# Linear attention in token order, with DMA transposes and one pool of 28 buffers

## The chip, the cores and the metric

The kernel runs on one core of a Trainium2 chip. The metric is the device time of one execution in microseconds (us); the median of three runs of the kernel before is 790.57 us (790.43 to 791.24). All data are bfloat16 in and out, sums are float32.

## The reference

Four layers follow each other on 2048 tokens of 576 values: linear attention, MLP, attention, MLP, each with a layer norm in front and a residual around it. Both attentions share their weights, and so do both MLPs.

```python
def _A_ref(x, wqkv, wo):                      # 32 heads of 18
    qkv = (x @ wqkv) -> q, k, v
    phi = lambda t: where(t > 0, t + 1, exp(t)) + 1e-6
    kv = einsum("bhsd,bhse->bhde", phi(k), v)
    z = einsum("bhsd->bhd", phi(k))
    num = einsum("bhqd,bhde->bhqe", phi(q), kv)
    den = einsum("bhqd,bhd->bhq", phi(q), z)[..., None] + 1e-6
    return (num / den) reshaped to tokens x 576, @ wo
def _B_ref(x, w1, b1, w2, b2):                # 576 -> 4608 -> 576
    h = gelu(layernorm(x) @ w1 + b1)
    return h @ w2 + b2
x = x + _A_ref(layernorm(x)); x = x + _B_ref(layernorm(x))    # and once more
```

## The kernel before, in words

Tokens are worked on in 16 tiles of 128. All weights stay on chip; the rows x between layers go through a DRAM buffer x_d and come back into rings (x_ring).

**LN pipe.** LNPipe (lines 220 to 308) takes each tile through statistics (DVE), a power on GpSimd for 1/sigma, the normalised row y (DVE, GpSimd), and then five TensorE transposes into PSUM (line 297) and one copy (lines 299, 301) into yT, which holds the normalised tokens with the 576 values along the partitions. Every call of tick() moves each tile one stage on.

**Attention, layer_A (358 to 534).** Front half, per token tile: k (line 370) and v (382, 385) in token order, phi of k in two ScalarE passes (319, 321) and two DVE steps (322, 324), and the sum of kv over all tiles (400). q is computed in channel order, a group of 7 heads by 512 tokens at a time (406). z comes out of a ones column of v. Second half: kv is masked to its heads (429, 433), multiplied into wo (451), the denominators of four tiles come from short matmuls (466, 470), their reciprocals (474) are spread over the channels by a matmul (482), copied (484) and multiplied into phi(q) (485). The output product (493) then takes scaled phi(q) and kv-wo; residual() (342) adds x and stores the row.

**MLP, LayerB (545 to 651).** Four chunks of 512 tokens. The first product makes 36 blocks of 128 hidden channels in 9 groups of four (m1_group, 553). TensorE runs two 64-row halves at once: the upper half takes the blocks in the order 0, 1, 2, 3, the lower 2, 3, 0, 1. The 64 rows left over of the 576 (w_tail) add one matmul to one half of every block, so that block 0 is complete one step before block 2. evict (586) reads a complete block with ScalarE's GELU into hT; that of block 3 is held back into the next group. Two tiny ScalarE copies per group (relay, 598) keep the two halves from meeting in one PSUM bank. Where the four blocks lie:

```python
hps = [ps_h.tile([P, 512], F32, name="h_ps", tag="h") for _ in range(2)]
pair = ps_acc.tile([P, 2, 512], F32, name="hp_ps", tag=next_acc())
dst = [hps[0][:], pair[:, 0, :], hps[1][:], pair[:, 1, :]]
```

The second product (640) sums 36 blocks by 2 halves for each of the chunk's four tiles; while it runs, the next chunk's rows (or the next attention's) are normalised and transposed, one tile for each tick.

**What sets the order.** A scheduler lays out each engine's instructions and places the semaphore waits by the tiles that they read and write. pe() chains TensorE's instructions to the program's order in the MLP and the front half of attention. All DMAs are issued by SP, in one queue, in order.

Of the kernel before, what the change touches and what calls it, by code (L numbers as in the profile page):

```python
# [17 lines left out]
KD = 5  # L18
# [5 lines left out]
GO = [126 * g for g in range(G)]  # L24
EPS = 1e-5
# [6 lines left out]
C1 = 1.0 + 1e-6  # L32


def build(tc, A_x, A_wqkv, A_wo, B_w1, B_b1, B_w2, B_b2, out, dbg=None, n_layers=4):
    nc = tc.nc
    dbg = dbg or {}
    with ExitStack() as ctx:
        const = ctx.enter_context(tc.tile_pool(name="const", bufs=1))
        ps_h = ctx.enter_context(tc.tile_pool(name="ps_h", bufs=3, space=PSUM))  # L40
        ps_tp = ctx.enter_context(tc.tile_pool(name="ps_tp", bufs=1, space=PSUM))
        ps_acc = ctx.enter_context(tc.tile_pool(name="ps_acc", bufs=1, space=PSUM))
        dpool = ctx.enter_context(tc.tile_pool(name="dram", bufs=1, space=DRAM))

# [13 lines left out]
        maskz = const.tile([P, 7, DH], F32, name="maskz")  # L58
        head_sel = const.tile([P, G, H], BF16, name="head_sel")
        head_bc = const.tile([P, G, P], BF16, name="head_bc")  # L60
        quad_mask = const.tile([P, 4, P], BF16, name="quad_mask")
        z_row = const.tile([P, 1], BF16, name="z_row")
        eps_row = const.tile([1, H], BF16, name="eps_row")
        one_row = const.tile([1, P], BF16, name="one_row")
        act_dummy = const.tile([P, 1], F32, name="act_dummy")

        def select(tile_, fill, op, base, pattern, mult):
            return lambda: nc.gpsimd.affine_select(out=tile_, in_=tile_, compare_op=op, fill=fill, base=base,
                                                   pattern=pattern, channel_multiplier=mult)

        def fill(tile_, value):
            return lambda: nc.gpsimd.memset(tile_[:], value)

        def inner_diag(tile_, lead, n):
            return [fill(tile_, 1.0),
                    select(tile_[:], 0.0, ALU.is_ge, 0, lead(1) + [[-DH, n]] + ([[0, DH]] if tile_ is maskz else []), 1),
                    select(tile_[:], 0.0, ALU.is_ge, DH - 1,
                           lead(-1) + [[DH, n]] + ([[0, DH]] if tile_ is maskz else []), -1)]

        hb = head_bc[:, :, 0:126].rearrange("p g (h d) -> p g h d", h=7)  # L80
        mask_steps = inner_diag(maskz, lambda sign: [], 7) + [
            select(maskz[:], 1.0, ALU.not_equal, -126, [[0, 7], [0, DH]], 1),
            fill(z_row, 0.0),
            select(z_row[:], 1.0, ALU.not_equal, -126, [[0, 1]], 1),
            fill(eps_row, 1e-6),
            fill(one_row, 1.0),
        ] + inner_diag(head_sel, lambda sign: [[126 * sign, G]], H) + [
            fill(quad_mask, 1.0),
            select(quad_mask[:], 0.0, ALU.is_ge, 0, [[-32, 4], [0, P]], 1),
            select(quad_mask[:], 0.0, ALU.is_ge, 31, [[32, 4], [0, P]], -1),  # L90
            fill(head_bc, 0.0),
        ] + [select(hb, 1.0, ALU.not_equal, -32 * quad, [[-7, G], [-1, 7], [0, DH]], 1) for quad in range(4)]
# [7 lines left out]
        wo_sb = const.tile([126, G, D], BF16, name="wo_sb")  # L100
# [6 lines left out]
        kvT = const.tile([P, G, 126], BF16, name="kvT")  # L107
        zsel = const.tile([P, G, H], BF16, name="zsel")
        NY = 4
        y_ring = [const.tile([P, DPAD], BF16, name=f"y_ring{i}") for i in range(NY)]  # L110
        NV = 3
        v_ring = [const.tile([P, G, P], BF16, name=f"v_ring{i}") for i in range(NV)]
        NX = 5
        x_ring = [const.tile([P, D], F32, name=f"x_ring{i}") for i in range(NX)]
# [3 lines left out]
        blk = ctx.enter_context(tc.tile_pool(name="blk", bufs=NF))  # L118

        x0_tiles = {}  # L120
# [13 lines left out]
        pe_chain = dict(on=False, last=None)  # L134

        def pe(inst):
            if pe_chain["on"]:
                if pe_chain["last"] is not None:
                    tc.add_manual_dep(inst.ins, pe_chain["last"], NOSYNC, reason="TensorE order in the MLP")
                pe_chain["last"] = inst.ins.name  # L140
            return inst

        def load_x0(t):
            x0 = blk.tile([P, D], BF16, name="x0", tag="blk")
            chained(nc.sync.dma_start(out=x0[:], in_=x_in[t * P:(t + 1) * P, :]))
            x0_tiles[t] = x0
# [18 lines left out]
        for i in (NY - 1, 0, 1, 2):  # L165
            nc.vector.memset(y_ring[i][:], 0.0)
        warm_ps = ps_h.tile([P, 512], F32, name="warm_ps", tag="h")

        def warm_pe(n):
            for _ in range(n):  # L170
                pe(nc.tensor.matmul(warm_ps[:], lhsT=y_ring[NY - 1][:, 0:P], rhs=y_ring[NY - 1][:, 0:512],  # L171
                                    start=True, stop=True))
# [3 lines left out]
        for vr in v_ring:  # L176
            nc.gpsimd.memset(vr[:, 4, 72:126], 0.0)
            nc.gpsimd.memset(vr[:, :, 126:127], 1.0)
            nc.gpsimd.memset(vr[:, :, 127:128], 0.0)

        def piece_wo():
            chained(nc.sync.dma_start(out=wo_sb[:, 0:4, :], in_=A_wo[0:504, :].rearrange("(g p) n -> p g n", p=126)))
            chained(nc.sync.dma_start(out=wo_sb[0:72, 4, :], in_=A_wo[504:D, :]))
# [32 lines left out]
        state = dict(ycnt=0, vcnt=0, xl=0)  # L216
        pool_last = dict(norm=None)
        dve_last = dict(norm=None, sum=None, phi=None)

        class LNPipe:  # L220
# [3 lines left out]
            def feed(self, xt, t, kind, norm_eng, evac_eng="dve", load_from=None, after=None):  # L224
                self.items.append(dict(stage=(0 if load_from is None else -1), xt=xt, t=t, kind=kind,
                                       norm=norm_eng, evac=evac_eng, load=load_from,
                                       after=after))

            def busy(self):
                return len(self.items)  # L230

            def tick(self, transposes=1):
                for it in list(self.items):
                    st = it["stage"]
                    if st == 4:
                        if transposes == 0:
                            continue
                        transposes -= 1
                    if st == -1:
                        xn = x_ring[3 + state["xl"] % 2]  # L240
                        state["xl"] += 1
                        load = nc.sync.dma_start(out=xn[:], in_=x_d[it["load"]])
                        if it["after"] is not None:
                            tc.add_manual_dep(load.ins, it["after"], NOSYNC, reason="loads give way")
                        it["xt"] = xn
                    elif st == 0:
                        xt = it["xt"]
                        stt = work.tile([P, 2, 6], F32, name="ln_st", bufs=4)
                        first = nc.vector.bn_stats(out=stt[:, 0, :], in_=xt[:, 0:HALF])
                        second = nc.vector.bn_stats(out=stt[:, 1, :], in_=xt[:, HALF:D])  # L250
                        if it["after"] is not None:
                            for stats in (first, second):
                                tc.add_manual_dep(stats.ins, it["after"], NOSYNC, reason="statistics give way")
                        mv = work.tile([P, 2], F32, name="ln_mv", bufs=6)
                        nc.vector.bn_aggr(out=mv[:], in_=stt[:])
                        u = work.tile([P, 1], F32, name="ln_u", bufs=4)
                        if it["kind"] == "A":
                            nc.vector.tensor_scalar(out=u[:], in0=mv[:, 1:2], scalar1=EPS, scalar2=None, op0=ALU.add)  # L258
                        else:
                            nc.vector.tensor_scalar(out=u[:], in0=mv[:, 1:2], scalar1=1.0 + EPS, scalar2=EPS * EPS,  # L260
                                                    op0=ALU.mult, op1=ALU.add)
                        it["mv"], it["u"] = mv, u
                    elif st == 1:
                        rstd = work.tile([P, 1], F32, name="ln_rstd", bufs=6)
                        nc.gpsimd.tensor_tensor(out=rstd[:], in0=it["u"][:], in1=neg_half[:], op=ALU.pow)  # L265
                        it["rstd"] = rstd
                    elif st == 2 and it["norm"] != "dve":
                        nmr = work.tile([P, 1], F32, name="ln_nmr", bufs=4)
# [89 lines left out]
        def layer_A(li, next_kind, pre_a1=None):  # L358
# [55 lines left out]
            for t in range(NT):  # L414
                if t != 1 or li > 0:
                    k_proj(t)
# [257 lines left out]
        def pre_a1_layer0(t):  # L674
# [6 lines left out]
            if t >= 4:  # L681
                masks(2)
# [73 lines left out]
```

## Time and profile before

| | |
|---|---|
| median of three runs | 790.57 us |
| profiled execution, span | 790.0 us |
| TensorE (PE) busy | 778.6 us, 99% |
| ScalarE (ACT) busy | 341.2 us |
| VectorE (DVE) busy | 264.5 us |
| first attention, with start-up | 0 to 112.1 us |
| first MLP | 112.1 to 401.2 us |
| second attention | 401.2 to 501.2 us |
| second MLP | 501.2 to 786.5 us |

The span runs from the first to the last instruction of one execution; the run's time is 0.6 us above it. A group of instructions is one row: line, engine, operation, output and inputs, shapes, count, busy time, mean duration in ns, and the idle time of the engine ahead of it with what ended most of it. The chain of waits follows the work back from the last instruction.

### The profile page before, as it was taken

How to read it: one execution, taken by the hardware profiler on the slowest of the kernel's cores; microseconds unless marked ns; L12 is line 12 of the kernel's file. 1: busy time of each engine (PE TensorE's matmuls, PEld its weight loads, DVE VectorE, ACT ScalarE, POOL GpSimd, SP SyncE). 2: the span in 40 equal slices, each digit the busy share in tenths (PEclk: the TensorE clock that was granted, in tenths of full speed). 3: DMA queues.
4: the chain of work that ended last, by engine and by line, in shares of the span. 5: the costliest groups of instructions: out<-in, count | busy, mean ns of one | idle time of the engine just before them, and what ended most of it. 6: DMA issues, size and time to landing. Idle time of an engine off the chain costs nothing.

```text
span 790.0 us, 16121 instructions
## 1 busy us (share of the span) xinstructions
PE 778.6 (99%) x6807; PEld 507.0 (64%) x6813; DVE 264.5 (33%) x711; ACT 341.2 (43%) x754; POOL 125.7 (16%) x211
## 2 busy tenths in 40 slices
PE   8999999999999999999999999999999999999998
PEld 5776654685478458646887766547745864685476
DVE  6786862135023504300344478433200300010000
ACT  5888646304610660164047785471066017304600
POOL 4571402013010301200100004211110110001000
PEclk9999999999999999999999999999999999999999
DMA  9990372012021202200210007611210110011000
GB/s 274 259 285 24 129 260 71 1 62 90 1 61 46 76 2 75 76 1 1 80 42 1 2 16 240 240 47 53 61 39 3 60 61 1 9 46 38 2 23 23
DMA packets 43506, 56.92 MB, mean 72 GB/s; under 512 B 10283, under 2 KB 28075, under 8 KB 43435
## 3 DMA queue, kind: packets, MB, share of 16 engines
q1 hardware_dynamic: 43434, 55.91, 23.1%
q8 instruction: 53, 0.87, 0.5%
q14 instruction: 19, 0.15, 0.1%
HBM read 39.38 MB, written 16.52 MB: 71 GB/s over the span
## 4 chain that ended last, share of the span: by engine, by line
PE 92%; DVE 4%; DMA 2%; ACT 1%; issue 1%; POOL 0%; DVEq 0%; POOLq 0%; ACTq 0%
PE m_ps L640 36%; PE h_ps L593 20%; PE hp_ps L593 16%; PE q_ps L406 5%; PE k_ps L370 5%; PE v_ps L385 3%; PE tp L297 2%; PE v_ps L382 2%; PE wo_ps L493 2%; DMA x_d<-xn 2%; DVE xn L349 1%; PE kvacc L400 1%; PE warm_ps L171 1%; DVE pq L485 1%; DVE rden L474 0%
## 5 line engine op out<-in xcount | busy, mean ns | idle before, releaser
L640 PE MATMUL m_ps<-w_sb,hT 128*128 128x288 bf16 x2304 | 289.9, 286 | 0.0
L640 PEld LDWEIGHTS <-hT 128*128 128x128 bf16 x2304 | 223.2, 98 | 57.9 <-issue 3.4
L593 PEld LDWEIGHTS <-w_sb 64*128 64x128 bf16 x2304 | 124.5, 94 | 136.5 <-issue 1.9
L593 PE MATMUL hp_ps<-yT,w_sb 64*128 64x512 bf16 x1152 | 178.0, 376 | 0.0
L593 PE MATMUL h_ps<-yT,w_sb 64*128 64x512 bf16 x1152 | 148.0, 376 | 0.0
L598 ACT COPY relay_sb<-relay_sb 128x1 f32<-128x1 f32 x144 | 28.5, 198 | 276.3 <-PE h_ps L593 234.2
L589 ACT ACTIVATE hT<-h_ps,b1T 128x512 bf16<-128x512 f32 x144 | 91.0, 683 | 44.5 <-PE h_ps L593 44.5
L301 DVE COPY yT<-tp 128x640 bf16<-128x640 bf16 x40 | 19.6, 490 | 239.5 <-PE tp L297 239.5
L265 POOL TENSOR_TENSOR ln_rstd<-ln_u,neg_half 128x1 f32<-128x1 f32 x64 | 36.0, 562 | 357.5 <-DVE ln_u L258 193.5
L589 ACT ACTIVATE hT<-hp_ps,b1T 128x512 bf16<-128x512 f32 x144 | 91.1, 692 | 0.0
L339 POOL TENSOR_TENSOR x_ring<-x_ring,b_bc 128x576 f32<-128x576 f32 x32 | 40.8, 1279 | 159.5 <-DMA x_ring<-x_d 159.5
L593 PE MATMUL h_ps<-yT,w_tail 64*128 64x512 bf16 x144 | 54.1, 376 | 0.0
L593 PE MATMUL hp_ps<-yT,w_tail 64*128 64x512 bf16 x144 | 54.1, 376 | 0.0
L349 DVE TENSOR_TENSOR xbf<-m_ps,x_ring 128x576 bf16<-128x576 f32 x16 | 12.0, 752 | 117.6 <-PE m_ps L640 117.6
L406 PE MATMUL q_ps<-yT,wqkv_sb 128*126 128x512 bf16 (+1 forms) x200 | 50.0, 382 | 0.5 <-ACT phi_a L321 0.5
L493 PE MATMUL wo_ps<-kvwo,pq 126*128 126x288 bf16 (+1 forms) x320 | 43.8, 285 | 3.5 <-DVE xn L349 3.0
L370 PE MATMUL k_ps<-wqkv_sb,yT 128*128 128x288 bf16 x320 | 44.3, 286 | 0.0
L319 ACT ACTIVATE phi_e<-k_ps 128x288 bf16<-128x288 f32 x64 | 27.0, 422 | 35.9 <-PE k_ps L370 35.8
L493 PEld LDWEIGHTS <-pq 126*128 126x128 bf16 (+1 forms) x320 | 30.6, 97 | 14.8 <-issue 5.0
L322 DVE TENSOR_SCALAR phi_e<-phi_e 128x288 bf16<-128x288 bf16 (+2 forms) x104 | 30.7, 295 | 27.3 <-ACT phi_e L319 26.9
L593 PEld LDWEIGHTS <-w_tail 64*128 64x128 bf16 x288 | 27.1, 94 | 17.1
L370 PEld LDWEIGHTS <-yT 128*128 128x128 bf16 x320 | 30.9, 98 | 11.1
(90 smaller groups left out, 643.6 us busy)
## 6 DMA issues: line engine op xcount, KB each, us to landing
x_ring<-x_d SPq DMA_DIRECT2D x72, 288.0 KB, 3.0
x_d<-xn SPq DMA_DIRECT2D x48, 288.0 KB, 2.2
w_sb<-in_B_w_dram SPq DMA_DIRECT2D x6, 864.0 KB, 10.4
w_sb<-in_B_w_dram SPq DMA_DIRECT2D x9, 512.0 KB, 5.3
x<-in_A_x_dram SPq DMA_DIRECT2D x16, 144.0 KB, 4.1
x_ring<-in_A_x_dram SPq DMA_DIRECT2D x16, 144.0 KB, 3.2
out_dram<-xbf SPq DMA_DIRECT2D x16, 144.0 KB, 1.8
wqkv_sb<-in_A_wqkv_dram SPq DMA_DIRECT2D x3, 576.0 KB, 5.8
```

The lines of the kernel that those rows point to most:

```text
L265: nc.gpsimd.tensor_tensor(out=rstd[:], in0=it["u"][:], in1=neg_half[:], op=ALU.pow)
L319: act_last["exp"] = nc.scalar.activation(out=e[0:rows, 0:n], in_=ps_ap, func=ACT.Exp).ins.name
L322: nc.vector.tensor_scalar(out=e[0:rows, 0:n], in0=e[0:rows, 0:n], scalar1=1.0, scalar2=1e-6, op0=ALU.min, op1=ALU.add)
L339: nc.gpsimd.tensor_tensor(out=xo, in0=xo, in1=b2_bc[:], op=ALU.add)
L370: pe(nc.tensor.matmul(kp[:, 0:HALF], lhsT=yT[:, k, tok], rhs=wqkv_sb[:, k, D + half * HALF: D + (half + 1) * HALF], start=(k == 0), stop=( ...
L385: pe(nc.tensor.matmul(vp[:, 1, 0:324], lhsT=yT[:, k, tok], rhs=wqkv_sb[:, k, 2 * D + 252: 3 * D], start=(k == 0), stop=(k == KD - 1)))
L406: pe(nc.tensor.matmul(qp[0:GR[g], :], lhsT=wqkv_sb[:, k, GO[g]:GO[g] + GR[g]], rhs=yT[:, k, c * CA:(c + 1) * CA], start=(k == 0), stop=(k ...
L493: pe(nc.tensor.matmul(wp[:, half, 0:HALF], lhsT=pq[(g, c)][0:GR[g], j * P:(j + 1) * P], rhs=kvwo[g][0:GR[g], half * HALF:(half + 1) * HALF ...
L589: act_last["gelu"] = nc.scalar.activation(out=hT[f][:, 0:CB], in_=dst[n], func=ACT.Gelu_apprx_tanh, bias=b1T[:, f:f + 1], scale=1.0).ins.name
L593: mm = pe(nc.tensor.matmul(dst[n], lhsT=wt, rhs=mv, start=(seen[n] == 0), stop=(seen[n] == 8)))
L598: relay = nc.scalar.copy(out=relay_sb[:, 1:2], in_=relay_sb[:, 0:1])
L640: pe(nc.tensor.matmul(acc[:, half, 0:HALF], lhsT=hT[f][:, j * P:(j + 1) * P], rhs=w2_sb[:, f, half * HALF:(half + 1) * HALF], start=(f == ...
```

## The change

The attention's second half works in token order, numerators LEAD (4) tiles ahead of the output product. v gets a ones column per head (19 columns a head, DZ), so that one product gives numerator and denominator of a token tile; the quotient is taken straight from PSUM, and the row is transposed by a DMA into yT, where the output product with the plain wo reads it. q is computed for two groups at a time, phi works on two PSUM banks at once.

```diff
+            def num_den(t):
+                c, j = divmod(t, TPC)
+                nd = next_pair()
+                for g in range(G):
...
+                        pe(nc.tensor.matmul(nd[:, lo // HB, at:at + (hi - lo) * DZ], lhsT=q_rows(g, c, j),
+                                            rhs=kvz[0:GR[g], lo * DZ:hi * DZ], start=True, stop=True))
+                heads = nd[:, :, 0:HB * DZ].rearrange("p b (h e) -> p b h e", e=DZ)
+                den = work.tile([P, 2, HB], F32, name="den", bufs=3)
+                nc.scalar.activation(out=den[:], in_=heads[:, :, :, DH], func=ACT.Identity, bias=1e-6, scale=1.0)
+                rden = work.tile([P, 2, HB], F32, name="rden", bufs=3)
+                nc.vector.reciprocal(out=rden[:], in_=den[:])
+                o = y_slot()
+                nc.vector.tensor_tensor(out=o[:, 0:D].rearrange("p (b h e) -> p b h e", b=2, h=HB),
+                                        in0=heads[:, :, :, 0:DH],
+                                        in1=rden[:].unsqueeze(3).to_broadcast([P, 2, HB, DH]), op=ALU.mult)
+                nc.sync.dma_start_transpose(out=yT[:, :, t * P:(t + 1) * P], in_=o[:])
...
+            num_den(0)
+            num_den(1)
+            q_two(*later.pop(0))
+            num_den(2)
+            num_den(3)
+            q_two(*later.pop(0))
             for t in range(NT):
...
                 wo_stage(t)
+                if t + LEAD < NT:
+                    num_den(t + LEAD)
+                if t in (1, 3):
+                    q_two(*later.pop(0))
```

The LN rows of all but the first layer are transposed by DMA too, and the statistics of the first four tiles of each MLP are two ScalarE passes with a running sum in place of DVE's:

```diff
+            if evac_eng == "dma":
+                nc.sync.dma_start_transpose(out=yT[:, :, t * P:(t + 1) * P], in_=y[:])
+                return
```

PSUM is now four fixed tiles of two banks each, for all stages, and the MLP's blocks lie in two of them per group:

```diff
-        ps_h = ctx.enter_context(tc.tile_pool(name="ps_h", bufs=3, space=PSUM))
-        ps_tp = ctx.enter_context(tc.tile_pool(name="ps_tp", bufs=1, space=PSUM))
-        ps_acc = ctx.enter_context(tc.tile_pool(name="ps_acc", bufs=1, space=PSUM))
+        psum = ctx.enter_context(tc.tile_pool(name="psum", bufs=1, space=PSUM))
+        pair = [psum.tile([P, 2, 512], F32, name=f"ps{i}") for i in range(4)]
...
-                hps = [ps_h.tile([P, 512], F32, name="h_ps", tag="h") for _ in range(2)]
-                pair = ps_acc.tile([P, 2, 512], F32, name="hp_ps", tag=next_acc())
-                dst = [hps[0][:], pair[:, 0, :], hps[1][:], pair[:, 1, :]]
+                turn["n"] ^= 2
+                banks = pair[turn["n"]], pair[turn["n"] + 1]
+                dst = [banks[n % 2][:, n // 2, :] for n in range(GF)]
...
-                    hT[f] = blk.tile([P, D], BF16, name="hT", tag="blk")
-                    act_last["gelu"] = nc.scalar.activation(out=hT[f][:, 0:CB], in_=dst[n], func=ACT.Gelu_apprx_tanh,
+                    if f // 2 not in homes:
+                        homes[f // 2] = two_tile("hT")
+                    hT[f] = homes[f // 2][:, (f % 2) * CB:(f % 2 + 1) * CB]
+                    act_last["gelu"] = nc.scalar.activation(out=hT[f], in_=dst[n], func=ACT.Gelu_apprx_tanh,
```

One pool of 28 buffers of 2304 bytes (two_tile, row_tile) holds input rows, pk, phi(q), phi's second half, hT by twos and the loaded rows. Rows that the next layer needs first stay on chip (tiles 0 to 3 from attention to MLP, 12 to 15 from MLP to attention); the first layer's input rows stay until their residual, and the second attention loads the others AHEAD (8) tiles ahead. pe() chains TensorE's instructions everywhere.

## The prediction

> **What bounds the kernel now.** I read the page's busy times and chain first, then the stages one by one.
>
> ```profile
> span 790.0 us, 16121 instructions
> PE 778.6 (99%) x6807; PEld 507.0 (64%) x6813; DVE 264.5 (33%) x711; ACT 341.2 (43%) x754; POOL 125.7 (16%) x211
> PE 92%; DVE 4%; DMA 2%; ACT 1%; issue 1%; POOL 0%; DVEq 0%; POOLq 0%; ACTq 0%
> ```
>
> TensorE has work for 99% of the span and holds 92% of the chain. So an instruction taken off TensorE is a gain, and a wait put into its queue is a loss at full price. From the chain's list in order of time I take the stages: first attention to 112.1 us, first MLP to 401.2, second attention to 501.2, second MLP to 786.5, then 3.5 of tail. The table of stretches shows how full they are (columns: stretch, us, busy us of PE, PEld, DVE, ACT, POOL; clock, DMA share, GB/s):
>
> ```profile
> 78.00:95.00 17.00, 16.48 (x130) 10.82 (x131) 16.13 (x45) 11.64 (x22) 6.19 (x10) 1.00 0.31 102
> 95.00:112.10 17.10, 15.54 (x142) 10.95 (x142) 11.75 (x22) 7.45 (x13) 3.50 (x7) 1.00 0.73 238
> 112.10:147.20 35.10, 35.10 (x326) 15.71 (x326) 7.71 (x21) 22.94 (x52) 6.88 (x11) 1.00 0.30 94
> 481.00:501.20 20.20, 17.87 (x160) 12.55 (x160) 14.05 (x30) 9.18 (x16) 4.61 (x8) 1.00 0.82 277
> ```
>
> The first product of an MLP chunk (112.1 to 147.2) has no idle TensorE at all; the only slack is about 2 us at the end of each attention.
>
> **MLP: what goes.** On the chain, normalised rows are transposed inside the second product:
>
> ```profile
> 221.17 0.28 PE tp L297 x5
> 221.45 2.94 PE m_ps L640 x24
> 224.39 0.28 PE tp L297 x5
> 224.67 2.94 PE m_ps L640 x24
> ```
>
> Five transposes take 0.28 us between matmuls. All 26 such tiles of the first MLP and 12 of the second go to DMA: 38 x 0.28 = **-10.6 us**. What takes their place, one DMA per tile, has the rest of the second product to land in, tens of us before the chunk that reads the row, so it is hidden; for the next attention's last tiles the cover is its first k and v products, 2.5 us a tile.
>
> **MLP: what is added.** Before, the four blocks of a group (line 562) lie in h_ps, pair half 0, another h_ps, pair half 1. After, blocks 0 and 2 are the halves of one tile, 1 and 3 of another. Block 0 gets its last matmul one step before block 2 gets its own (the w_tail piece), and block 0's GELU is issued in between. In the built order of the changed program exactly that w_tail matmul of block 2 waits for ScalarE, on the count that block 0's GELU raises, in 72 of 72 groups (9 groups, 4 chunks, 2 MLPs). In the built order of before none of these matmuls waits for ScalarE. Reader and writer are in different halves, but of one tile now. The price comes from these rows:
>
> ```profile
> L593 PE MATMUL h_ps<-yT,w_tail 64*128 64x512 bf16 x144 | 54.1, 376 | 0.0
> L589 ACT ACTIVATE hT<-h_ps,b1T 128x512 bf16<-128x512 f32 x144 | 91.0, 683 | 44.5 <-PE h_ps L593 44.5
> 115.16 1.26 ACT L589 ACTIVATE hT<-h_ps,b1T 128x512 bf16<-128x512 f32 x2 [0.68 <-PE h_ps L593]
> ```
>
> The first is a matmul's 376 ns, the second the GELU's 683 ns and that it starts upon a matmul. A matmul of this shape starts 0.216 us after the one before (35.07 us for 162 pairs). After: block 0's last matmul ends at 0.376 us, ScalarE starts 0.05 later (0.04 to 0.10 by its start times against matmul ends), takes 0.683, and TensorE goes on 0.05 later (the gap between phi_a and the q_ps matmul that waits for it at 468.77): 1.16 instead of 0.216, **0.95 us per group**. ScalarE has no backlog then: in the third row it had stood idle 0.68. Behind the wait stand all later matmuls, so nothing hides it: 72 x 0.95 = **+68.4 us**. Bounds: 0.75 (only the GELU and the two hand-offs, should the matmul's end be modelled late), 54 us, and 1.1, 79 us.
>
> The Trainium skill, "PSUM — Partial Sum Buffer", section Terms, forbids two engines the same bank at once, which two different halves are not. By that rule the wait protects nothing and 68.4 would be 0; but the wait is in the program, and no trace here shows a wait that is written being skipped.
>
> **Attention: work.** Removed per layer, by TensorE start-to-start times: denominators 4 x 0.56, quotient broadcasts 20 x 0.216, kv-wo products 10 x 0.123, z 0.5, transposes 4 x 0.28 (8 in the second layer): 9.4 and 10.5 us. Added: six short matmuls per token tile. They have 38 to 133 columns; the 128-column transposes and the kv products (126) go at 0.056 to 0.058, so 16 x 6 x 0.056 = 5.4. Projections and the output product keep their columns. Net **-4.0 and -5.1**. If the idle 2 and 3 us of before go too (they end on DVE xn and behind it DMA x_d<-xn, a ring of three that the pool of 28 replaces), -6 and -8.
>
> **Attention: waits.** (a) The masks of kvz now stand bare between the last kv product and the first numerator: L429's 676 ns for 504 columns gives 0.6 + 0.3 + 0.2, about 1.2 us of idle TensorE. (b) The new loop per tile: ScalarE takes denominators (0.23), DVE a reciprocal (L474: 948 ns for 128 columns, so some 0.35 for 32; bounds 0.15, the shortest DVE rows, and 0.95), the quotient (as xn, 0.75), SP a transpose, and the output product four tiles later. DVE per tile is 0.75 + 0.35 + 0.75 less 0.08 overlap each, 1.6, against TensorE's 1.23 + 0.34 = 1.57: even, about +2 with the GELU table load and phi passes between. (c) SP takes its queue in order, and in the built order the LN transposes of tiles 0 to 3 (for the MLP) stand among the quotients': LN 0 before quotient 5, LN 1 before 6, LN 3 before 8. An LN row needs two ScalarE passes (0.65 each), five short GpSimd steps (0.5 each), the norm (0.89) and pad copy (0.26): 5 us after its residual if nothing is in the way, but GpSimd also adds b2 to kept rows in that stretch (L339, 1.28 each), and phi passes of 2 us stand between the two ScalarE passes. For LN 3 that makes 10 us after its product. Quotient 8 is issued only then, and lands 3 us later, while its product was due 8 us after product 3: a stall of **5**. The same behind LN 0 to 2, shorter: about **4** together. Sum of (a) to (c): +12 per layer. In the first layer's front half q and transposes share a pair and k has one home: waits of 0.1 us on ScalarE in ten tiles each, **+2**. Balance with the idle of before gone: -6 + 12 + 2 = **+8**, -8 + 12 = **+4**. Bounds: -14 for both layers (no stall), +24 (twice the stalls).
>
> **The DMA transpose itself** has no row. A store of nearly its size (out_dram, 144 KB) takes SP 0.34 us and lands in 1.8; a load in 256-byte pieces (w_tail) 0.60 of SP; the load in single elements (b1_raw) 3.09. The built instruction works in pieces of 16 x 128, 40 of them, so I take 1.0 on SP and 3 to landing, nearer to w_tail; ends 0.34 and 3.09. Per tile SP then has 1.0 + 0.32 for a store, below TensorE's 1.57. At 0.34 the stalls shrink by 3 to 5 us in all; above about 1.7 SP sets the pace and each further 0.1 costs 20 transposes x 2 layers x 0.1 = 4 us, +30 to 50 at 2.5 to 3.09.
>
> **Sum**, against the profiled execution: 790.0 - 10.6 + 68.4 + 8 + 4 = 859.8. The median shown, 790.57, is 0.6 above the span: **860 us**.
>
> **Rivals.** (1) *DMA transposes set the pace of attention.* For it: 20 in a row on one queue, no row that shows one. Against: each moves less than an x_d store, which lands in 2.2. At 2.5 us each, 860 + 33 = 893; at 5, 20 x 5 + 9 = 109 us instead of some 46 (34 of TensorE's work and 12 of waits) per second half: 985. The Trainium skill, "VectorE: DVE Perf Modes", section The three transpose paths, gives 1309 ns for a 128 x 128 block by DMA; five blocks would be 6.5 us (an estimate from that page) and the kernel about 1040. "DMA: Bandwidth & Descriptors", section Latency and other measured facts, has 261 GB/s, an estimate of 0.6 us, and leaves 860. No run here shows either; to times beyond 985 I give 0.04 of this rival's chance.
> (2) *Faster: the 72 waits are over before TensorE reaches them.* The place is the w_tail matmul, the price 0.95 each. For it: ScalarE is idle a third of the first product (22.94 of 35.10 busy). Against: the GELU waited for starts only upon the matmul one step earlier. With 0 per group, 791.5 with attention's stalls as above, 766 without; taking attention midway (-1), the time is below 790.6 if the wait costs under (10.6 + 1) / 72 = 0.16 us.
> (3) *The change doesn't relieve attention's TensorE at all* (stalls twice as long, +24): 872, inside the forecast.
>
> **Chances.** Forecast 0.74, rival 1 0.20, rival 2 0.05, other 0.01. Range: low 790.6 - 10.6 + 68.4 - 14 = 834, less likely than the middle, so 838; high to rival 1's milder end, 893. Faster by over 0.2% (what a measurement of this kernel can tell) 0.04, within 0.01, slower 0.95.
>
> **What would show it.** In the profile after: TensorE idle of 65 to 70 us put down to ScalarE's hT on the group line (L591), some 0.95 x 72; first-product stretches of 43.6 us and second-product ones of 35.3 without tp; in both attentions idle on DMA yT before the output product, one stall near tile 8, and transposes of about 1 us on SP. Wrong would be: no idle at L591 (rival 2), or transposes over 2 us and most of the loss in attention (rival 1).

## The result, and the profile after

The changed kernel takes 862.85 us (median of 4 runs, 862.18 to 863.22) against 790.79 us for the kernel before on the same chip: ratio 1.0911, 95% interval 1.0895 to 1.0926. It is slower by 72 us; the forecast was 860 (838 to 893).

The head of the page after:

```profile
span 860.5 us, 15498 instructions
PE 776.2 (90%) x6503; PEld 514.3 (60%) x6503; DVE 225.7 (26%) x521; ACT 339.0 (39%) x666; POOL 115.8 (13%) x206
```

TensorE has 304 matmuls fewer and is busy 2.4 us less than the 778.6 before, but the span is 70.5 longer: time is lost to idle TensorE, from 11 us before (790.0 - 778.6) to 84 us after. Its waits in the trace after say upon what (us in total, times, the longest):

```profile
PE ps L591 <- ACT hT L587: 56.4, 72, 0.8
PE ps L511 <- DMA yT<-y_ring: 13.1, 8, 4.6
PE ps L494 <- ACT phi_a L314: 2.7, 2, 1.4
PE ps L511 <- DVE y_ring L502: 2.4, 3, 1.1
```

The first row is the MLP: 72 waits on a GELU, one per group. The second is attention's output product waiting for a transposed quotient to land. The groups of the page show both sides of the first row (busy us, mean ns, and idle time ahead with what ended it):

```profile
L591 PE MATMUL ps<-yT,w_tail 64*128 64x512 bf16 x288 | 108.0, 375 | 56.4 <-ACT hT L587 56.4
L587 ACT ACTIVATE hT<-ps,b1T 128x512 bf16<-128x512 f32 x288 | 190.0, 685 | 92.0 <-PE ps L591 89.6
```

Of the 288 w_tail matmuls 72 carry the 56.4 us, 0.78 each; and ScalarE is idle ahead of its GELUs, so there was no backlog: the GELU starts when the matmul lets it, and TensorE stands still for its length. One period of the chain of waits, second MLP:

```profile
548.16 0.02 issue
548.18 0.70 ACT hT L587
548.88 0.04 issue
548.92 4.08 PE ps L591 x36
```

It adds up to 4.84 us for a group, against 3.90 before (the chain of before has the nine groups of a chunk from 112.14 to 147.21 us, 35.07 / 9): 0.94 for each group, 72 x 0.94 = 67.7. The 0.94 is more than the 0.78 shown as idle, because the matmul in front of a wait runs to its end (0.375) where otherwise the next one would start 0.216 after it. The stretches of the first MLP's first chunk (columns as before):

```profile
119.71:163.36 43.65, 36.66 (x325) 17.82 (x325) 7.49 (x21) 25.03 (x52) 3.14 (x8) 1.00 0.21 56
163.36:198.75 35.39, 35.39 (x292) 28.10 (x290) 7.56 (x18) 1.26 (x2) 1.64 (x3) 1.00 0.18 40
```

The first product takes 43.65 where it took 35.10; the second one is full.

In attention, the one long wait is at tile 8. The row of the output product, and SP's queue before it:

```profile
105.21 2.35 PE L511 MATMUL ps<-wo_sb,yT 128*128 128x288 bf16 x10 [4.61 <-DMA yT<-y_ring]
```

```profile
98.72 0.53 SPq L356 DMA_DIRECT2D x_d<-xn  x1
100.58 1.22 SPq L268 DMA_TRANSPOSE yT<-y_ring  x1
101.89 0.53 SPq L356 DMA_DIRECT2D x_d<-xn  x1
102.52 1.24 SPq L505 DMA_TRANSPOSE yT<-y_ring  x1
```

Quotient 8 left DVE at 98.32 by the timeline. SP stood before the LN row of tile 3 (L268), whose last GpSimd step ended at 100.56, and only then came a store and the quotient (L505). It landed at 105.2. A DMA transpose takes 1.2 us of SP here, and 2.6 to its landing:

```profile
L505 SPq DMA_TRANSPOSE yT<-y_ring x32: 1199/1224/1326, 76.5 to 536.3; - x32
yT<-y_ring SPq DMA_TRANSPOSE x80, 2.6
```

### The profile page after: what moved, and what is told of

It is laid out like the page before. It is cut to its first block, busy times and chain, and to the rows that moved or that the text cites. A ratio compares the mean times of both kernels' runs of the same rounds, so it can differ in the third digit from the quotient of the medians.

```text
span 860.5 us, 15498 instructions
## 1 busy us (share of the span) xinstructions
PE 776.2 (90%) x6503; PEld 514.3 (60%) x6503; DVE 225.7 (26%) x521; ACT 339.0 (39%) x666; POOL 115.8 (13%) x206
## 5 line engine op out<-in xcount | busy, mean ns | idle before, releaser
L591 PE MATMUL ps<-yT,w_sb 64*128 64x512 bf16 x2304 | 293.2, 376 | 0.0
L637 PE MATMUL ps<-w_sb,hT 128*128 128x288 bf16 x2304 | 283.6, 286 | 0.0
L591 PEld LDWEIGHTS <-w_sb 64*128 64x128 bf16 x2304 | 131.9, 94 | 190.5 <-issue 79.6
L587 ACT ACTIVATE hT<-ps,b1T 128x512 bf16<-128x512 f32 x288 | 190.0, 685 | 92.0 <-PE ps L591 89.6
L591 PE MATMUL ps<-yT,w_tail 64*128 64x512 bf16 x288 | 108.0, 375 | 56.4 <-ACT hT L587 56.4
L330 POOL TENSOR_TENSOR xo<-xo,b_bc 128x576 f32<-128x576 f32 x28 | 35.5, 1275 | 206.3 <-DMA xo<-x_d 197.1
L511 PE MATMUL ps<-wo_sb,yT 128*128 128x288 bf16 x320 | 47.2, 297 | 15.6 <-DMA yT<-y_ring 13.1
L419 PE MATMUL ps<-yT,wqkv_sb 128*126 128x512 bf16 (+1 forms) x200 | 47.5, 380 | 0.1
L511 PEld LDWEIGHTS <-yT 128*128 128x128 bf16 x320 | 30.4, 101 | 27.3 <-DMA yT<-y_ring 15.9
L400 PE MATMUL ps<-wqkv_sb,yT 128*128 128x288 bf16 x320 | 44.4, 286 | 0.5 <-ACT v_ring L403 0.5
L388 PE MATMUL ps<-wqkv_sb,yT 128*128 128x288 bf16 x320 | 44.3, 286 | 0.1
L314 ACT ACTIVATE phi_a<-ps 128x576 bf16<-128x576 f32 (+4 forms) x57 | 41.9, 735 | 0.0
L388 PEld LDWEIGHTS <-yT 128*128 128x128 bf16 x320 | 30.4, 98 | 10.0 <-ACT yT L274 0.2
L591 PEld LDWEIGHTS <-w_tail 64*128 64x128 bf16 x288 | 27.1, 94 | 15.0
L400 PEld LDWEIGHTS <-yT 128*128 128x128 bf16 x320 | 30.8, 98 | 7.8 <-issue 0.6
```

The lines of the kernel that those rows point to most:

```text
L314: act_last["phi"] = nc.scalar.activation(out=a3, in_=ps, func=ACT.Identity, bias=C1, scale=1.0).ins.name
L330: nc.gpsimd.tensor_tensor(out=row[:], in0=row[:], in1=b2_bc[:], op=ALU.add)
L388: pe(nc.tensor.matmul(dst[:, half, 0:HALF], lhsT=yT[:, k, tok], rhs=wqkv_sb[:, k, D + half * HALF: D + (half + 1) * HALF], start=(k == 0), ...
L400: pe(nc.tensor.matmul(vp[:, half, 0:HALF], lhsT=yT[:, k, tok], rhs=wqkv_sb[:, k, 2 * D + half * HALF: 2 * D + (half + 1) * HALF], start=(k ...
L419: pe(nc.tensor.matmul(bank[0:GR[g], :], lhsT=wqkv_sb[:, k, GO[g]:GO[g] + GR[g]], rhs=yT[:, k, c * CA:(c + 1) * CA], start=(k == 0), stop=( ...
L511: pe(nc.tensor.matmul(wp[:, half, 0:HALF], lhsT=yT[:, k, t * P:(t + 1) * P], rhs=wo_sb[:, k, half * HALF:(half + 1) * HALF], start=(k == 0 ...
```

## The experiments

All were timed against the kernel before on the same chip, whose medians were 790.5 to 790.7.

**1. The MLP's wait, taken away.** Block 0's GELU is issued after block 2's last matmul, just ahead of block 2's own GELU; the tiles stay as the change has them.

```diff
-                    if seen[n] == 9 and n != 3:
+                    if seen[n] == 9 and n in (1, 2):
+                        if n == 2:
+                            evict(0)
                         evict(n)
```

> The changed kernel with one edit: the GELU of block 0 is issued together with that of block 2, behind block 2's last matmul, so that no matmul of the group is left that would wait for it. Theory (the 72 waits cost 0.94 us each): 862.9 - 72 x 0.94 = 795, and no idle time of TensorE put down to hT; what is left over the 790.8 of before is attention's. Rival (the first product is slower for another reason, such as the two-bank tiles or hT by twos): a smaller fall, at the extreme none, 863.

Measured: 793.68 us, ratio 1.0037 (1.0024 to 1.0051). No wait on hT is left; the first row of TensorE's waits is now attention's:

```profile
PE ps L511 <- DMA yT<-y_ring: 13.2, 9, 4.7
```

So 862.85 - 793.68 = 69.2 us of the change's loss is this one wait, and a reordering of one ScalarE instruction per group undoes it.

**2. The wait alone, put into the kernel before.** Blocks 0 and 2 are made halves of one tile; nothing else is touched.

```diff
-                dst = [hps[0][:], pair[:, 0, :], hps[1][:], pair[:, 1, :]]
+                dst = [pair[:, 0, :], hps[0][:], pair[:, 1, :], hps[1][:]]
```

> The kernel before with one line changed: blocks 0 and 2 of a group take the two halves of the pair, blocks 1 and 3 the two single tiles; nothing else of the change is in it. Theory (it is the shared tile that makes the w_tail matmul wait for block 0's GELU): 790.8 + 72 x 0.94 = 858.5, with TensorE's idle time on hT 72 times. Rival (the wait needs the new fixed PSUM tiles or the new pool): 791.

Measured: 858.71 us, ratio 1.0858 (1.0842 to 1.0874).

```profile
PE hp_ps L593 <- ACT hT L589: 55.2, 71, 0.8
```

A permutation of four names costs 858.71 - 790.66 = 68.1 us. The same number from both sides.

**3. What one wait is made of.** The pass that is waited for is cut to 256 of the 512 columns; the other half of block 0 is evicted behind block 2's last matmul.

```diff
...
-                    if seen[n] == 9 and n != 3:
+                    if seen[n] == 9 and n == 0:
+                        evict(0, slice(0, CB // 2))
+                    if seen[n] == 9 and n in (1, 2):
+                        if n == 2:
+                            evict(0, slice(CB // 2, CB))
                         evict(n)
```

> The changed kernel, but the pass that the third block's last matmuls wait for covers only the first 256 of its 512 columns; the other half is evicted behind the third block's last matmul. The 72 waits stay, on a pass of about half the length. The GELU pass takes 685 ns for 512 columns; a pass of 256 columns takes, by the elements, about 685/2 + 60 = 400 ns at most 450. Theory (the price of a wait is the length of the pass waited for, plus the two semaphore steps): each of the 72 is 0.24 to 0.34 us shorter, 17 to 24 us in sum, 863 - 17 to 24 = 839 to 846, and the mean wait by the trace falls from 0.78 to 0.45 to 0.55 us. Rival (the price is a fixed one of waiting, refilling the pipeline and the semaphores, whatever the pass): 860 to 864, waits still 0.75 to 0.8.

Measured: 848.24 us, ratio 1.0725 (1.0709 to 1.0741): 14.6 us less, or 0.20 for each wait. It is less than the 17 to 24 expected, and the rows say why:

```profile
PE ps L591 <- ACT hT L587: 41.3, 72, 0.9
L587 ACT ACTIVATE hT<-ps,b1T 128x256 bf16<-128x256 f32 x144 | 68.3, 474 | 78.3 <-PE ps L591 77.7 <-DMA x_d<-xn 0.6
```

The half pass takes 474 ns, not 400 to 450: a pass has some 260 ns that don't shrink (474 x 2 - 685). The wait is the pass plus a constant: 0.57 - 0.47 = 0.10 here, 0.78 - 0.69 = 0.09 in the whole one. So the wait follows the length of the pass at both lengths tried; my size for the half pass was off.

**4. The MLP's gain alone.** In the kernel before, the rows normalised inside the MLPs are transposed by DMA.

```diff
+                        if it["evac"] == "dma":
+                            nc.sync.dma_start_transpose(out=yT[:, :, t * P:(t + 1) * P], in_=y[:])
+                            self.items.remove(it)
+                            continue
...
-                        lnp.feed(None, t, "B", "dve", "dve", load_from=t, after=(dve_last["sum"] if c == 0 else None))
+                        lnp.feed(None, t, "B", "dve", "dma", load_from=t, after=(dve_last["sum"] if c == 0 else None))
...
-                            lnp.feed(xn, t, "A", "dve", "dve")
+                            lnp.feed(xn, t, "A", "dve", "dma")
```

> The kernel before with one part of the change alone: the rows that an MLP normalises (its own later chunks, and those for the next attention) are transposed by DMA; tiles 0 to 3 of each MLP and the first attention stay on TensorE, PSUM and attention are as before. Theory (38 tiles x 0.28 us leave TensorE, the DMA, 1.2 us on SP and 2.6 to landing, is hidden): 790.8 - 10.6 = 780. Rival (the transposes delay the loads and stores that stand behind them in SP's queue, or land too late for the chunk): 788 to 795.

Measured: 779.70 us, ratio 0.9860 (0.9845 to 0.9874). This is the fastest of all the versions: 11.0 us less, for work on a queue that nothing waits for. With experiment 1 it splits the change: -11.0 for the MLPs' rows, 793.68 - 779.70 = +14.0 for attention in its new form, +69.2 for the wait. The three add up by construction. What bears the split out is that the MLP stages of the two traces are equally long (281.75 and 281.98 us in experiment 1, 281.74 and 281.90 here), so that the +14.0 lies in the two attentions.

**5. All rows by DMA in the kernel before.** As 4, and the rows of tiles 0 to 3 in attention too (`"act"` becomes `"dma"` in layer_A's feed).

> The kernel before with all rows transposed by DMA, those of tiles 0 to 3 in attention too (the run with only the rows in the MLPs by DMA gave 779.7). Eight more row tiles leave TensorE: 8 x 0.28 = 2.2 us. Theory (SP has room in the attention of before, where no quotient waits on it): 777 to 778. Rival (the rows' transposes, 1.2 us each, and the stores before them on SP come late for the first product of the MLP behind it, or they hold up what SP brings attention): 780 to 783.

Measured: 783.52 us, ratio 0.9909 (0.9893 to 0.9926): 3.8 us worse than 4, in place of 2.2 better. Attention's output product now waits longer for VectorE's residual (L353). It writes a ring of three rows that stores on SP set free, and SP's queue has the transposes now. The trace fits: before L353 VectorE stands idle 8.1 us until a store x_d<-xn has landed, 4.1 in experiment 4. No run tried it apart.

```profile
PE wo_ps L497 <- DVE xn L353: 6.0, 8, 1.3
```

In experiment 4 that row was 1.8 us. The 4.2 us more, 2.2 of work less, and one stretch of half clock (last section; about 1.7 us) make 3.7. A transpose on DMA was free in the MLP, where its queue has nothing urgent behind it, and not in attention. The changed kernel has these eight transposes on DMA too, so their cost is part of the +14.0.

**6. Attention without the rows' transposes on SP.** What the next MLP reads for tiles 0 to 3 is left out.

```diff
                 yield
+            if stats == "act":
+                return
             yield "transpose"
```

> The changed kernel without the four DMA transposes of tiles 0 to 3 for each MLP, those that stand among the quotients' in SP's queue; left out with them is the MLP's input of these 512 tokens, for which it reads what lies in yT. Theory (these four hold up the quotient of tile 8): the stall of 4.6 us and the 1.7 us that the matmuls behind it lose at half clock vanish in both layers, some small ones with them: 862.9 - 2 x 6.5 = 850, down to 848. Rival (SP's 1.2 us a transpose, or DVE, sets the pace, and the stall only moves): 857 or more.

Measured: 857.03 us, ratio 1.0837 (1.0819 to 1.0855), 5.8 us less than the changed kernel, where the first theory had 13. The stall of 4.6 has gone, but not the waiting:

```profile
PE ps L513 <- DMA yT<-y_ring: 7.2, 12, 1.4
```

Twelve short waits take the place of eight. What is late next could be SP, which now takes some 1.95 us for a tile's transpose and store, or VectorE. In a stretch of the changed kernel where TensorE does not wait, its tiles follow each other after 1.52 us (numerators and output product), and VectorE's after 1.78 (residual, reciprocal and quotient; it is busy 5.02 of 5.40 us from 109.8 to 115.2):

```profile
109.89 1.39 PE L511 MATMUL ps<-wo_sb,yT 128*128 128x288 bf16 x10
111.41 1.39 PE L511 MATMUL ps<-wo_sb,yT 128*128 128x288 bf16 x10
109.80 0.76 DVE L347 TENSOR_TENSOR xn<-ps,x 128x576 f32<-128x576 f32 x1
111.58 0.75 DVE L347 TENSOR_TENSOR xn<-ps,x 128x576 f32<-128x576 f32 x1
```

(The 1.84 us for TensorE's tile in the expectations of experiments 9 and 10 adds two rows, 1.39 + 0.45, that overlap.) So SP and VectorE both take longer for a tile than TensorE there. Experiments 7 and 8 ask about SP; no run asks about VectorE.

**7. The order on SP.** The rows' transposes are tied to follow the latest quotient (a scheduling order, no semaphore).

```diff
-                nc.sync.dma_start_transpose(out=yT[:, :, t * P:(t + 1) * P], in_=y[:])
+                rows = nc.sync.dma_start_transpose(out=yT[:, :, t * P:(t + 1) * P], in_=y[:])
+                if stats == "act":
+                    tc.add_manual_dep(rows.ins, dma_last["quotient"], NOSYNC, reason="MLP rows give way to quotients")
```

> The changed kernel, but in attention the DMA transposes of the next MLP's first four row tiles are issued on SP behind the quotient transposes that were ready before them. Theory A (the order on SP is the cause of the stall of 4.6 us at tile 8, as the prediction's step (c) had it): both stalls and the half clock behind them go, 2 x (4.6 + 1.7) = 12.6, and 863 - 12.6 = about 850, with no wait on a quotient's DMA over 1.5 us. Theory B (SP's own time sets the pace, 1.22 us for each of 20 transposes and 0.5 us for each store per layer, whatever their order): the waits are only dealt out differently, 859 to 863, with the sum of the waits on quotient DMAs still 8 us or more.

Measured: 866.50 us, ratio 1.0960 (1.0944 to 1.0977), 3.6 us slower than the changed kernel. The order alone is not the cause; SP's queue in this run has no gap from 99 us on:

```profile
100.36 0.53 SPq L359 DMA_DIRECT2D x_d<-xn  x1
101.00 1.22 SPq L508 DMA_TRANSPOSE yT<-y_ring  x1
102.33 1.22 SPq L269 DMA_TRANSPOSE yT<-y_ring  x1
```

Each entry starts about 0.1 us after the end of the one before, and the longest wait on a quotient is 3.4, four tiles later. Theory A is out; B said 859 to 863, and it came out dearer.

**8. SP relieved.** As 6 (the same inputs left out), with attention's 24 stores issued by ScalarE.

```diff
-                nc.sync.dma_start(out=x_d[t], in_=dst)
+                (nc.scalar if li % 2 == 0 else nc.sync).dma_start(out=x_d[t], in_=dst)
```

> The changed kernel without the transposes of the next MLP's first four row tiles (those MLP inputs are left out, as in the run without row transposes in attention, 857.0), and with attention's stores of rows issued by ScalarE and no longer by SP. SP then issues only the quotient transposes, 1.24 us per tile where it had 1.9 with the store. Theory B (SP's time sets attention's pace): the 12 waits of 7.2 us on quotient DMAs go nearly all, 857.0 - 5 to 7 = 850 to 852. Rival (what is left of them is the latency of DVE's quotients and of the transfer, or ScalarE's evictions come later by its 0.5 us stores): 855 to 859.

Measured: 857.37 us, ratio 1.0850 (1.0834 to 1.0867), the same as 6. A gain of 5 to 7 us did not come, so theory B falls here. One thing could hide a gain: each store now takes ScalarE 0.33 us, and no run separates that. The execution that was profiled took 859.28 us, the longest of the four:

```profile
PE ps L513 <- DMA yT<-y_ring: 9.4, 12, 2.4
```

SP now issues most quotients (25 of 32) within 0.2 us of VectorE's last step, and still the waits stay. I followed the longest one through the timeline of this run: tile 8's numerators start at 93.10; its denominators leave ScalarE at 95.88, behind two phi passes; VectorE ends the quotient at 99.03, behind a phi step and two residuals; SP issues at 99.18; and the output product starts at 103.51, 4.3 us later, which is the longest landing of this run where the median is 2.7, at a time when the DMA engines are busy throughout (share 1.03 from 100.0 to 103.4). That is 10.4 us. What TensorE has to do in between is its own 0.3 us of numerators and three tiles, 3 x 1.52 = 4.6, so about 4.9 (the expectation for experiment 9 has 7.4, with four tiles of 1.84).

**9. and 10. A longer lead.** On top of experiment 1, the quotients run six tiles ahead; in 10 the stores are ScalarE's as well (the diff of 8).

```diff
-LEAD = 4
+LEAD = 6
...
             num_den(3)
             q_two(*later.pop(0))
+            num_den(4)
+            num_den(5)
```

> The changed kernel with the first block's GELU behind its own last matmul (the run with the GELU after the tail, 793.7), and in attention the quotients' matmuls six tiles ahead of the output projection and no longer four. Theory C (what the two attention layers still lose is latency: from a tile's quotient matmul over ScalarE, VectorE, SP's 1.2 us and the transfer to the landing is about 7.5 us where the cover of four tiles is 4 x 1.84 = 7.4): the cover becomes 11.0 us, the 13.2 us of waits on quotient DMAs fall below 5, and with them the half clock behind the two long ones (2 x 1.7): 793.7 - 8 to 12 = 782 to 786. Rival (SP's or VectorE's throughput sets the pace, so that a longer lead only moves the waits): 791 to 795.

> The kernel of the run with a lead of six tiles, and attention's 24 stores of rows issued by ScalarE and no longer by SP. If SP's throughput takes part in what is left (1.22 us for a transpose and 0.5 us for a store per tile against 1.84 us of TensorE, and 1.2 us more for each of four row tiles), the time falls by 2 to 5 us below the run without this edit; if only latency counted, it is the same within 1 us, or later by up to 1 us for ScalarE's own issues (0.33 us each).

Measured: 791.03 us, ratio 1.0006 (0.9997 to 1.0016), and 792.02, ratio 1.0025 (1.0014 to 1.0036). The lead takes 2.7 us off the 793.68, which is in the rival's range; the stores from ScalarE bring nothing and cost 1.0. The cover became five tiles, about 7.9 us by the 1.52, and not 11.0. TensorE's waits with the lead of six:

```profile
PE ps L494 <- DVE y_ring L502: 6.9, 6, 1.8
PE ps L494 <- ACT phi_a L314: 5.1, 4, 1.3
PE ps L511 <- DMA yT<-y_ring: 3.3, 6, 0.6
```

The waits on DMA fell from 13.2 to 3.3 as theory C said, but the numerators (L494) now wait 12.0 us, where it was 2.6 on phi_a and none on the quotient: the four PSUM tiles come back only when VectorE has taken a quotient or ScalarE a phi. The wait changed its place.

**11. The quotients turned by TensorE.** On top of experiment 1, and otherwise in token order.

```diff
-                nc.sync.dma_start_transpose(out=yT[:, :, t * P:(t + 1) * P], in_=o[:])
+                quotient[t] = o
+            def rows_of(t):
+                o = quotient.pop(t)
+                tp = next_pair()[:, 0, 0:DPAD // 2].bitcast(BF16).rearrange("p (k n) -> p k n", k=KD)
+                for k in range(KD):
+                    pe(nc.tensor.transpose(out=tp[:, k, :], in_=o[:, k * P:(k + 1) * P], identity=ident[:]))
+                nc.scalar.copy(out=yT[:, :, t * P:(t + 1) * P], in_=tp)
...
+                if t + 2 < NT:
+                    rows_of(t + 2)
```

> The changed kernel with the first block's GELU behind its own last matmul (793.7), and the quotients turned by TensorE (five 128 x 128 transposes, a copy out of PSUM by ScalarE) two tiles ahead of the output projection, and no longer by DMA; the rest of attention in token order stays. Added on TensorE: 32 tiles x 0.28 = 9.0 us; gone: the waits on quotient DMAs, 13.2, and the half clock behind two of them, 2 x 1.7. Theory (what attention loses is the way over SP and the transfer): 793.7 + 9.0 - 16.6 = 786, 784 to 789. Rival (VectorE's and ScalarE's part of the chain and the four PSUM pairs set the pace, and a third user of the pairs makes that worse): 797 or more, with the waits on the quotients' and the phis' release of PSUM grown by what the DMA waits lose.

Measured: 793.36 us, ratio 1.0035 (1.0021 to 1.0049), the same as the 793.68 with the DMA. Neither number was expected. TensorE is busy 6.2 us more (769.2 against 763.0: 9.0 of transposes, less 2 x 1.7 for two stretches of half clock, would be 5.6), its waits on DMA are gone, and in their place stands

```profile
PE ps L519 <- ACT phi_a L314: 8.9, 4, 3.2
```

The output product (L519 here) waits until ScalarE's phi passes have read the PSUM tile that it is to write: the transposes are a third user of the four tiles. In this attention the way of the quotient's transpose is an even trade.

## Why the prediction was right, step by step

The forecast was the case that came, 860 for 862.85; the likeliest sum of the span, 859.8, met 860.5.

- **MLP rows off TensorE, -10.6.** Measured alone -11.0 (experiment 4). The two MLP stages get 7.25 and 3.35 us shorter there, 10.6 in sum, as the 38 tiles said; that the transposes on DMA are hidden was right. In all 40 row tiles leave TensorE (200 matmuls fewer on the page of experiment 4); the other two are transposed at the start of the second attention, where the prediction counted four (its "8 in the second layer" is 6 by the trace of before).
- **The wait on block 0's GELU, +68.4.** Measured 69.2 and 68.1 (experiments 1 and 2), 0.94 for each of 72 by the chain where 0.95 was worked out. Rival 2 (the wait is over by then) is refuted by the 72 rows. The sign that the prediction named was too high: 65 to 70 us of idle at L591 was expected and 56.4 is shown, because 0.16 of each 0.94 lies in the matmul that runs to its end, which counts as busy. The Trainium skill, "PSUM — Partial Sum Buffer", section Terms, speaks of two engines on the same bank. Here they were on two banks of one tile, and the trace has the wait all the same: this program's semaphores go by tiles (experiment 2).
- **Attention, +8 and +4.** By the starts of the stages +7.6 (the first MLP from 112.1 to 119.7) and +4.4 (the second attention 100.0 before, 104.4 after). The sums fit better than their terms, and in the first layer that is luck: 4 us less work and 12 more of idle TensorE were forecast, 0.6 less busy time (107.4 to 106.8) and 8.2 more idle time (4.7 to 12.9) were measured. In the second, 5.1 less and 9 more were forecast, 4.0 and 8.4 measured. In each, about 1.7 us of the busy time after is the half clock (last section), which the sum doesn't have. Of the waits, (c) was put at 9 a layer, and the waits on quotient DMAs are 5.8 and 7.4; (b) was put at 2, and the waits on phi, on the quotient and behind the table load are 3.4 and 3.0. The +2 in the first layer's front half did not come: TensorE is idle 1.1 us from 8 to 72.8 us after, and 1.3 from 8 to 78 before.
- **Attention alone.** Against the form of before the new one costs +14.0 (experiments 1 and 4), in which TensorE is busy 4.3 us less (763.0 against 767.3), the half clock included, and idle 17.9 more (27.9 against 10.0). The two measures, 14.0 and 7.6 + 4.4, differ by 2, and so does the second attention in the kernel of experiment 4: it takes 98.1 us there and 100.0 before, with 1.3 less idle time and 0.7 less work (two of the row tiles).
- **Step (c), SP's order.** The stall was forecast as 5 at tile 8 and is 4.6, by that order. As a cause it was incomplete: removing the transposes of tiles 0 to 3 gives back 5.8, reordering them nothing (experiments 6 and 7). Step (a), the bare masks, was 1.2 for each layer and is 1.0 (2.0 us of waits on kvz in both).
- **The DMA transpose, 1.0 on SP and 3 to landing.** Measured 1.2 and 2.6. Rival 1 at 2.5 us each did not come. The Trainium skill, "VectorE: DVE Perf Modes", section The three transpose paths, gives 1309 ns for one 128 x 128 block; here five such blocks land in 2.6 us, so its figure scaled by five does not hold for this form, as the trace decides.

What stays open: which of the four steps (ScalarE's denominators, VectorE's quotient, SP with the transfer, the release of PSUM) would have to shrink first for attention in token order to win. Experiments 8 to 11 moved SP's part, the lead, both, and the transfer, and each time another wait took over, within 3 us; VectorE's and ScalarE's own work was not shortened by any run. VectorE is the rival left standing: step (b) of the prediction had its tile even with TensorE's, 1.6 against 1.57, and the trace has 1.78 against 1.52 (experiment 6).

## What to carry to other kernels

Before the arithmetic of a layout, read which tile each accumulator lies in: two accumulators in one tile make the writer of one wait for the reader of the other, and the wait was the reader's whole pass plus about 0.1 us here, each time; an order in which the reader is issued after the last writer removes it. Work moved to a DMA queue was free where nothing urgent stands behind it on that queue (the MLP: -11.0), and not where stores that others wait for share the queue (attention before: +3.8). When a chain of four engines is as long as its cover, cutting one link can move the wait to the next, as in experiments 8 to 11: look for the sum of TensorE's idle time, not for one row of it.

## What the runs showed of the hardware

Not expected: the half clock after a stall (the granted clock is the share of full speed that the chip lets TensorE run at). In the changed kernel, the matmuls behind the 4.6 us stall run at a granted clock of 0.50, for 3.41 us; the table of stretches, first the 3.41 us before and then those:

```profile
102.07:105.48 3.41, 0.27 (x3) 0.23 (x4) 0.20 (x1) 0.00 (x0) 0.00 (x0) 1.00 0.86 222
105.48:108.90 3.42, 3.42 (x21) 2.34 (x19) 1.67 (x3) 0.20 (x1) 0.00 (x0) 0.50 0.84 212
```

It is not the length of one stall that decides. In experiment 5 no TensorE idle stretch in attention reaches 1.5 us, and still:

```profile
97.48:100.89 3.41, 1.62 (x12) 1.16 (x12) 2.41 (x6) 0.00 (x0) 2.37 (x5) 1.00 1.00 277
100.89:104.31 3.42, 3.42 (x15) 1.83 (x13) 2.81 (x6) 0.82 (x2) 0.00 (x0) 0.50 1.03 272
```

In every trace the stretches of full clock, up to the next half one, last a whole multiple of 3.413 us (in the changed kernel 416.43 us, 122 of them, between its two stalls; in experiment 11 785.07, 230 of them), so the clock changes on a grid. In the traces of twelve kernels here, from start-up to the last product, each stretch of that grid with 1.62 us of busy TensorE or less (47%) was followed by 3.41 us at half clock, and none with 1.66 or more (49%) was. Experiment 11 does not fit:

```profile
476.64:480.05 3.41, 1.45 (x15) 1.20 (x15) 2.28 (x5) 3.26 (x7) 2.90 (x6) 1.00 0.55 173
480.05:483.47 3.42, 2.90 (x22) 1.88 (x20) 2.47 (x4) 2.21 (x6) 2.05 (x6) 1.00 0.24 48
```

There TensorE was busy for 1.45 us (43%), and the clock stayed full. So a stretch less than half busy can bring the half clock, and did in all but this kernel, but busy time alone does not decide it; what does is open, and no run tried it. The price is about 1.7 us each time, twice in the changed kernel. The MLP's 72 waits cost no clock; TensorE is busy for 84% of the first product there (36.66 of 43.65). The Trainium skill, "TensorE: Matmul & The Clock Gate", section Part 1: The HAM clock gate, has the free-running window of 3413 ns and the half clock, and the traces agree with both; it says that an idle window brings the half clock, and the runs show that a window about half idle can.
